# Windowed attention and two feed-forward networks on one core: the networks' instructions ordered by the in-kernel list scheduler

## The chip, the cores and the metric

One Trainium2 chip, one core. The metric is device time in microseconds (us) of the whole kernel. All times before and after are medians of several executions; the profile is one more execution.

## The reference

Inputs are float32; the kernel holds what attention makes and what the networks make on the chip.

```python
scores = q @ k.T / 8 + bias                 # 4 batches, 8 heads, 576 rows, head size 64
scores = where(0 <= rel < 128, scores, -1e9)
attn   = softmax(scores);  x = attn @ v     # x: 2304 tokens x 512
h = x @ w_in;  g = h * sigmoid(1.702 * h);  x = g @ w_out          # network 1: 512 -> 2048 -> 512
h = x @ w_in;  g = h if h >= 1, 0 if h <= -1, else (h + 1)**2 / 4  # network 2
out = g @ w_out
```

The four weight matrices come as float64 and are read by the kernel as pairs of int32.

## The kernel before

**Number format.** Each float32 operand of a product is split in a high part (float32r) and a low part, and a product is three matmuls (high·high, high·low, low·high). A slice of weights (128 x 512 numbers) is loaded as int32 pairs (`load_raw`, L256), turned into float32 by five steps (`convert`, L269: one on ScalarE, four on VectorE, lines 271 to 282), and split (L316 or L764 the high part on ScalarE, `low_of`, L291, the low part on VectorE or GpSimd).

**First product (the h stage).** Tokens come in three blocks of 768 for each network, so there are six blocks (`blk` 0 to 5). The inner width of 2048 is 16 slices, taken in 8 pairs. A pair of slices and a block's two halves are multiplied by a scheme with 7 products in place of 8 (`product`, L344; 6 matmuls each, L348). For it a pair of weights is made into five pieces A, B, C, E, F: four sums on GpSimd (`sum_w`, L305), a high part (L316) and a low part (L291) each. Four PSUM banks X, Y, Z, V hold partial results that are copied or added (L813, L359), then go through the activation (L366 or L368) and a multiplication (L372, or L375 and L376), which gives the tiles `g`. Pair `q` runs over all six blocks, 0 to 47.

**Second product (the o stage).** For each of 16 slices and two halves, `g` is split (L871, L291) and multiplied by the slice of `w_out`: 12 matmuls for network 1 (L911), 9 wider ones for network 2 (L913).

**Weights are prepared once.** In block 0 the pieces of network 1 are made and stored in DRAM (`keep_piece`, L729), likewise the split slices of `w_out` (L766). Blocks 1, 2 and later load them (L726, L866). Network 2's weights are prepared the same way in blocks 1 and 2 (`prepare_in`, L770, and `prepare_out`, L756), with loads and stores on GpSimd's queue and their tiles in a pool `tmp` of four buffers. A tile written to DRAM frees its buffer when the store has landed.

**What sets the order.** Every engine executes its queue in order and stops at a head that waits. For attention and pair 0 the queues are written by a planner: `jobs` (L57) lists jobs with an engine, an occupancy, a latency, needs, buffers taken and given, and a key; `in_order` (L181) repeatedly takes the job that can start earliest. In that part 10 slices (`EARLY`) of `w_in` of network 1 are also converted and stored in DRAM (`plain`), and pair 0 is read back and split. Everything behind it is issued by program order in the loop from L928: `stage_h` makes pair `q+1` while pair `q` is multiplied (`make_w`, L738, reads `plain` back), `to_plain` (L751) converts the six late slices into `plain`, and `background` (L922) puts in pieces of network 2's preparation by a fixed credit of 4 us for a pair and 2.4 us for a slice.

Of the kernel before, what the change touches and what calls it, by code (L numbers as in the profile page):

```python
# [12 lines left out]
F32 = mybir.dt.float32  # L13
# [4 lines left out]
EARLY = 10  # L18
# [31 lines left out]
SLACK, AHEAD = 26, 12  # L50
# [6 lines left out]
def jobs(nu, n_heads2, early):  # L57
# [5 lines left out]
    def load(name, eng, n, ns, key, takes=()):  # L63
        add(name, eng, 640 * n, 640, key, takes=takes)
        add((name[0] + " landed", name[1]), "DMA", ns, ns + 2000, key, [name])
# [70 lines left out]
    key = KEYS["pair"][0]  # L136
    add(("rd", 0), "SP", 640, 640, key - 4, [("ws landed", 0), ("ws landed", 1)], [("wraw", "rd")])
    add(("rd landed", 0), "DMA", 2400, 4400, key - 4, [("rd", 0)])
    for i in range(4):
        add(("cs", i), "POOL", 700, 830, key, [("rd landed", 0)] + [("cs", i - 1)] * (i > 0), [("sum", "w")] * (2 * (i == 0)))  # L140
    for i, (n, needs) in enumerate(((512, []), (512, [("cs", 3)]), (256, [("cs", 2)]), (256, [("cs", 3)]), (256, []))):
        add(("ch", i), "ACT", 90 + n, 220 + n, key, [("rd landed", 0)] + needs)
        add(("cl", i), "DVE", 50 + n * 3 // 2, 170 + n * 3 // 2, key, [("ch", i)] + needs,
            gives=[("wraw", "rd")] * (i == 4) + [("sum", "w")] * (2 * (i == 3)))
    key = KEYS["xs"][0]
    ready = [(x, u) for u in range(2 * n_heads2) for x in ("x0", "x1")]
    for i in range(4):
        needs = (ready, [("xt", 0)], ready + [("xt", 3)], [("xt", 1)])[i]
        add(("xt", i), "POOL", 1850, 2000, key + KEYS["xs"][1] * (0, 1, 3, 2)[i], needs, [("sum", "x")])
    for i in range(7):  # L150
        needs = ready if i < 3 else [("xt", (3, 0, 1, 2)[i - 3])] + [("xt", 1)] * (i == 4) + [("xt", 3)] * (i == 5)
        add(("xh", i), "ACT", 840, 970, key + KEYS["xs"][2] + KEYS["xs"][3] * i, needs)
        add(("xl", i), XL_ENG[i], *XL_COST[XL_ENG[i]], key + KEYS["xs"][2] + KEYS["xs"][3] * i, needs + [("xh", i)],
            gives=[("sum", "x")] * (i > 2))
    key = KEYS["h"][0]
    chain = []
    for n, (i, bank, needs) in enumerate((
            (1, "X", []), (5, "W", []), (6, "X", [("hc", "Y")]), (2, "Y", [("hc", "Y")]), (7, "X", [("hc", "Z")]),
            (3, "Z", [("hc", "Z")]), (4, "V", [("hc", "V")]))):
        tile_, part = A_OF[i]  # L160
        add(("h", i), "PE", 1060, 1260, key + 0.1 * n, needs + [("xl", B_OF[i]), ("cl", PIECE[tile_, part])] + chain[-1:],
            [("s", bank)] * (i in (1, 5)))
        chain = [("h", i)]
    for bank, i, need in (("Y", 1, ("h", 1)), ("Z", 6, ("h", 5)), ("V", 7, ("hm", 11))):
        add(("hs", bank), "PE", 180, 380, key + 0.1 * i, [need], [("s", bank)])
        add(("hc", bank), "DVE" if bank == "Z" else "ACT", 500, 640, key + KEYS["h"][1],
            [("h", i), ("hs", bank)] + [("hc", "W")] * (bank == "Z"))
# [822 lines left out]
```

## Time and profile before

| | us |
|---|---|
| median of 3 runs | 1012.98 (1010.64 to 1013.78) |
| the profiled execution | 1011.4 |
| its span, first to last instruction | 1009.6 |
| TensorE busy | 901.0 (89%) |
| VectorE busy | 650.9 (64%) |
| ScalarE busy | 485.2 (48%) |
| GpSimd busy | 239.2 (24%) |
| bytes moved | 223.44 MB, mean 221 GB/s |

The chain that ended last names TensorE for 54% of the span, transfers for 12% and VectorE for 12%. In the 40 slices, TensorE stands at 9 tenths from slice 23 on and at 6 to 8 in most of slices 6 to 22. The granted clock is 9 in most slices and 7 or 8 in some of slices 6 to 20. A stretch's "busy" time on TensorE counts matmuls at the clock of the moment, so a slower clock makes it longer.

### The profile page before, as it was taken

How to read it: one execution, taken by the hardware profiler on the slowest of the kernel's cores; microseconds unless marked ns; L12 is line 12 of the kernel's file. 1: busy time of each engine (PE TensorE's matmuls, PEld its weight loads, DVE VectorE, ACT ScalarE, POOL GpSimd, SP SyncE). 2: the span in 40 equal slices, each digit the busy share in tenths (PEclk: the TensorE clock that was granted, in tenths of full speed). 3: DMA queues.
4: the chain of work that ended last, by engine and by line, in shares of the span. 5: the costliest groups of instructions: out<-in, count | busy, mean ns of one | idle time of the engine just before them, and what ended most of it. 6: DMA issues, size and time to landing. Idle time of an engine off the chain costs nothing.

```text
span 1009.6 us, 17030 instructions
## 1 busy us (share of the span) xinstructions
PE 901.0 (89%) x6009; PEld 821.7 (81%) x6009; DVE 650.9 (64%) x1455; ACT 485.2 (48%) x1162; POOL 239.2 (24%) x361
## 2 busy tenths in 40 slices
PE   8987967776987886988777999999999999999998
PEld 6866857665976886987777889999889988899886
DVE  8979887667896655566677962679226772277421
ACT  6978955454444444333444632545225452355322
POOL 5759872432234332233311100000000000000000
PEclk9999979877999988999899999999999999999999
DMA  9996467666677887667899863676448853486233
GB/s 200 211 205 184 127 225 265 245 238 242 245 242 266 286 293 275 227 211 251 293 346 367 274 231 125 223 247 203 136 136 279 255 191 125 167 265 214 84 126 126
DMA packets 134726, 223.44 MB, mean 221 GB/s; under 512 B 65136, under 2 KB 73584, under 8 KB 134640
## 3 DMA queue, kind: packets, MB, share of 16 engines
q1 hardware_dynamic: 121248, 181.83, 56.7%
q0 software_dynamic: 11136, 39.85, 10.7%
q10 hardware_dynamic: 2256, 0.66, 0.3%
q8 instruction: 48, 0.79, 0.3%
q14 instruction: 38, 0.31, 0.1%
HBM read 167.25 MB, written 55.05 MB: 220 GB/s over the span
## 4 chain that ended last, share of the span: by engine, by line
PE 54%; DMA 12%; DVE 12%; issue 11%; POOL 7%; ACT 4%; SPq 0%; POOLq 0%; ACTq 0%; DVEq 0%
PE b L348 23%; PE b L913 19%; PE b L911 6%; DMA raw<-in_moe_w_out_dram 4%; POOL tmp L305 3%; PE ps_t L561 2%; PE ps_s L514 2%; PE ps_x L587 1%; DVE x L279 1%; DVE x L282 1%; PE ps_qk L494 1%; DVE gs L291 1%; DVE x L276 1%; DMA r<-plain 1%; DVE x L273 1%
## 5 line engine op out<-in xcount | busy, mean ns | idle before, releaser
L911 PE MATMUL b<-gs,wo 128*128 128x384 f32 x1152 | 211.9, 341 | 26.3 <-ACT gs L871 11.7
L911 PEld LDWEIGHTS b<-gs,wo 128*128 128x128 f32 x1152 | 201.5, 190 | 36.2 <-ACT gs L871 16.9
L291 DVE TENSOR_TENSOR gs<-g,gs 128x384 fp32r<-128x384 f32 x192 | 114.4, 599 | 143.7 <-ACT gs L871 143.3
L913 PE MATMUL b<-wo,gs 128*128 128x512 f32 x864 | 196.4, 389 | 0.0
L913 PEld LDWEIGHTS b<-wo,gs 128*128 128x128 f32 x864 | 162.1, 188 | 33.6
L871 ACT CAST gs<-g 128x384 fp32r<-128x384 f32 x192 | 96.9, 513 | 178.2 <-PE b L913 129.5
L348 PE MATMUL b<-xs,wB 128*128 128x384 f32 x564 | 124.8, 360 | 35.5 <-ACT b L813 29.4
L348 PEld LDWEIGHTS b<-xs,wB 128*128 128x128 f32 x564 | 106.4, 203 | 43.0 <-ACT b L813 33.9
L348 PE MATMUL b<-xs,wA 128*128 128x384 f32 x564 | 121.6, 351 | 14.7 <-ACT wA L316 7.5
L348 PEld LDWEIGHTS b<-xs,wA 128*128 128x128 f32 x564 | 105.1, 199 | 17.9 <-ACT wA L316 8.8
L368 ACT ACTIVATE g<-b,half 128x384 f32<-128x384 f32 x96 | 55.5, 584 | 46.0 <-PE b L348 44.9
L375 DVE TENSOR_TENSOR m<-b,g 128x384 f32<-128x384 f32 x96 | 53.2, 557 | 37.9 <-ACT g L368 35.9
L549 POOL TENSOR_SCALAR p<-p,sm 128x192 f32<-128x192 f32 (+2 forms) x144 | 63.9, 462 | 35.8 <-DVE sm L525 15.4
L359 DVE TENSOR_TENSOR b<-b,m 128x384 f32<-128x384 f32 x94 | 52.5, 559 | 29.0 <-PE b L348 24.4
L348 PE MATMUL b<-xs,wE 128*128 128x384 f32 x282 | 69.1, 340 | 0.0
L348 PE MATMUL b<-xs,wC 128*128 128x384 f32 x282 | 59.2, 345 | 11.1 <-DVE b L359 11.0
L533 ACT ACTIVATE p<-p,sm 128x192 f32<-128x192 f32 (+2 forms) x144 | 62.3, 441 | 7.0 <-DVE sm L525 6.9
L348 PEld LDWEIGHTS b<-xs,wC 128*128 128x128 f32 x282 | 50.6, 193 | 14.0 <-DVE b L359 14.0
L813 ACT COPY b<-b 128x384 f32<-128x384 f32 x94 | 44.0, 470 | 36.3 <-PE b L348 36.0
L372 DVE TENSOR_TENSOR g<-b,g 128x384 f32<-128x384 f32 x92 | 50.1, 554 | 16.1 <-ACT g L366 15.7
L348 PE MATMUL b<-xs,wF 128*128 128x384 f32 x282 | 57.9, 340 | 1.2 <-ACT b L813 1.2
L316 ACT CAST tmp<-tmp 128x256 fp32r<-128x256 f32 (+1 forms) x40 | 19.7, 491 | 77.7 <-POOL tmp L305 21.9
(168 smaller groups left out, 1248.8 us busy)
## 6 DMA issues: line engine op xcount, KB each, us to landing
wo<-r SPq DMA_DIRECT2D x80, 512.0 KB, 3.3
raw<-in_moe_w_in_dram SPq DMA_DIRECT2D x16, 512.0 KB, 4.9
raw<-in_moe_w_out_dram SPq DMA_DIRECT2D x16, 512.0 KB, 3.7
r<-wo SPq DMA_DIRECT2D x16, 512.0 KB, 3.0
raw<-in_moe_w_in_dram POOLq DMA_DIRECT2D x16, 512.0 KB, 5.5
raw<-in_moe_w_out_dram POOLq DMA_DIRECT2D x16, 512.0 KB, 5.7
r<-tmp POOLq DMA_DIRECT2D x16, 512.0 KB, 6.0
out_dram<-xt SPq DMA_DIRECT2D x17, 256.0 KB, 2.2
```

The costliest lines, as they stand in the source:

```text
L291: eng.tensor_tensor(out=dst[:, 1], in0=src, in1=f32(dst[:, 0]), op=ALU.subtract)
L348: nc.tensor.matmul(bank, wc[name][:, a, part, k * P:(k + 1) * P], xs[B_OF[i]][:, b, k, :], start=(first and k == 0 and n == 0), stop=(last ...
L359: nc.vector.tensor_tensor(out=dst, in0=bank, in1=m5, op=ALU.add)
L368: nc.scalar.activation(g, bank, AF.Relu, scale=0.5, bias=half)
L372: nc.vector.tensor_tensor(out=g, in0=bank, in1=g, op=ALU.mult)
L375: nc.vector.tensor_tensor(out=t, in0=bank, in1=g, op=ALU.max)
L533: nc.scalar.activation(x, x, AF.Exp, bias=sm[:, 0, a, e:e + 1], scale=-1.0, accum_out=sm[:, 1, a, e:e + 1])
L549: nc.gpsimd.tensor_scalar(out=x, in0=x, scalar1=st[u]["sm", g][:, 2, a, e:e + 1], scalar2=1.0, op0=ALU.mult, op1=ALU.mult)
L813: nc.scalar.copy(b, banks_of[q]["X"])
L871: nc.scalar.copy(gs[:, 0], g)
L911: nc.tensor.matmul(o[m][:, 0:N], wo[:, a, sl], gs[:, b, :], start=start, stop=stop)
L913: nc.tensor.matmul(o[m], gs[:, b, sl], wo[:, a, :], start=start, stop=stop)
```

## The change

The loop from L928 with its helpers is gone. A new function `ffn_jobs` lists every operation and every transfer of the six blocks as jobs with costs, and one call of `in_order` orders attention and networks together; the result is issued job by job. TensorE's own order of products is fixed by the list (look-ahead 1) and is the order that the loop had. For the other queues the look-ahead is 150 jobs; jobs of the networks take shared buffers in the order of their keys, and none is put on an engine before that engine's attention jobs are all placed.

```diff
-EARLY = 10
+EARLY = 8
-SLACK, AHEAD = 26, 12
+SLACK, AHEAD, AHEAD2 = 0, 12, 150
+LATE, SLACK2 = 1000, 100
+CAPS2 = dict(b=8, tmp=3, xtmp=1, wo=3, gs=3, m5=2, craw=2, cx=2)
+W_WORK = (("ACT", 690, 850), ("DVE", 440, 620), ("DVE", 430, 610), ("DVE", 710, 890), ("DVE", 700, 880))
+def ffn_jobs(nf, nj, early):
...
+    def move(name, eng, kb, at, needs=(), takes=(), gives=()):
+        add(name, eng, 450 if eng == "SP" else 700, 700, at, needs, takes)
+        add((name[0] + " landed", *name[1:]), "DMA", kb * 3, kb * 3 + (2500 if eng == "SP" else 4000), at, [name], (), gives)
...
+                    eng, occ = ("POOL", 1850) if x == 1 else ("DVE", 1100)
+                    add(name, eng, occ, occ + 160, t + 5500 * n - 1500, ...)   # the four differences of a block of x
...
+            move(("lw", q, x), "SP", size[x], first - 15000, needs)
...
+            eng, hold = eng_of(i), ["tmp" if i < 2 else "cx"] * (n == 2)
+            add(("ch", q, i), "ACT", 110 + size_, 280 + size_, t(i), needs, hold)
+            add(("cl", q, i), eng, occ, occ + 160, t(i) + 600, needs + [("ch", q, i)] + ...)
+            move(("kp", n, q % hp, i), "SP" if n == 1 else "POOL", 512 if size_ == 512 else 256, t(i) + 1500, [("cl", q, i)], (), hold)
...
+    for q in range(2, hp):
+        t = at["h", q, 1]
+        landed = [("rd landed", q)]
+        if 2 * q < early:
+            move(("rd", q), "SP", 512, t - 16000, (), ["wo"])
+        else:
+            for a in range(2):
+                conversion(1, 0, 2 * q + a, t - 14000 + 2500 * a, ["wo"] * (a == 0), "SP")
+            landed = [("w4", 1, 0, 2 * q + a) for a in range(2)]
+        sums(q, t - 8000, landed, ["tmp"])
+        pieces(q, 1, ..., "wo", lambda i: "POOL" if i < 1 else "DVE", landed)
...
+    begin, until = at["h", hp, 1], at["h", nj * hp, 1] - 10000
+    step = (until - begin) / hp      # network 2's pairs and slices are spaced by it
...
 def in_order(todo, caps):
...
-            for j in queue[:AHEAD]:
+            for j in queue[:AHEAD if not queue or queue[0].key < LATE else 1 if eng == "PE" else AHEAD2]:
+                if j.key >= LATE > queue[0].key:
+                    break
...
+                if j.key >= LATE and any(turns[what][0] != j.name for what in counts):
+                    continue
-                if first is None or (t <= first[0] + SLACK if j.key < first[1].key else t < first[0] - SLACK):
+                slack = SLACK if j.key < LATE else SLACK2
+                if first is None or (t <= first[0] + slack if j.key < first[1].key else t < first[0] - slack):
                     first = (t, j)
```

Late slices of `w_in` of network 1 (8 to 15) are converted straight into the tile from which their pair is split, without `plain`. Pairs 0 and 1 are both read back, summed and split in attention; pair 1 takes the buffers of attention's `raw` and `v` tiles. The low part of piece B of network 1 moves from GpSimd to VectorE, and the four differences of x for block 1 from VectorE to GpSimd. One pool of eight 4 KB buffers and one of five 2 KB buffers serve attention and the networks alike:

```diff
+    quad = keep_pool("quad", CAPS["raw"] + CAPS["wraw"] + CAPS["sum"])
+    duo = keep_pool("duo", CAPS["v"] + CAPS["wx"])
...
+    def do_ch(q, i):
+        name = NAMES[i]
+        if q < HP:
+            wcs.setdefault(q, {})[name] = new_wc(q, name)
+        else:
+            wcs.setdefault(q, {})[name] = (four if PARTS[name] == 2 else two)([P, 2, PARTS[name], 256], F32R, "piece")
+        high_w(i, wcs[q], sums_w.get(q), raw_in[q])
...
         with tc.manual_schedule():
-            for _, (what, *args) in in_order(jobs(NU, NP, EARLY), CAPS):
-                if what in do:
-                    do[what](*args)
+            for name in order:
+                if keys[name] < LATE and name[0] in do:
+                    do[name[0]](*name[1:])
...
+    with tc.manual_schedule():
+        for name in order:
+            if keys[name] >= LATE and name[0] in do:
+                do[name[0]](*name[1:])
```

The planner's keys for attention (`KEYS`) have new numbers throughout; the planner's costs of attention's jobs are the same but for loads that read `plain` back.

## Rows read from the trace of the kernel before

**Rows 1.** The page's first line.

```profile
span 1009.6 us, 17030 instructions
```

**Rows 2.** Stages: length; busy us (instructions) of PE, PEld, DVE, ACT, POOL; clock; DMA share, GB/s.

```profile
0.00:134.50 134.50, 118.81 (x2015) 97.09 (x2015) 116.92 (x518) 111.31 (x414) 92.65 (x183) 0.99 0.80 186
134.50:234.50 100.00, 68.24 (x299) 60.70 (x298) 72.90 (x113) 49.10 (x105) 42.47 (x42) 0.82 0.71 258
234.50:317.60 83.10, 74.68 (x384) 68.92 (x385) 66.97 (x102) 33.52 (x65) 30.51 (x26) 0.95 0.67 232
317.60:403.80 86.20, 66.34 (x337) 63.60 (x337) 51.54 (x100) 40.59 (x91) 26.19 (x37) 0.90 0.81 285
403.80:481.60 77.80, 69.15 (x386) 66.28 (x386) 48.73 (x86) 27.54 (x57) 25.67 (x36) 1.00 0.67 229
481.60:565.20 83.60, 65.24 (x339) 62.04 (x337) 60.11 (x117) 44.38 (x94) 17.38 (x31) 0.94 0.95 341
565.20:634.40 69.20, 67.43 (x386) 66.47 (x385) 40.26 (x71) 22.93 (x44) 4.38 (x8) 1.00 0.56 187
634.40:692.80 58.40, 58.40 (x337) 58.22 (x337) 42.32 (x81) 33.22 (x64) 0.00 (x0) 1.00 0.76 245
```

**Rows 3.** TensorE's timeline, the last unbroken run of block 2's o stage.

```profile
602.22 32.16 PE L911 MATMUL b<-gs,wo 128*128 128x384 f32 x184 [1.56 <-DVE gs L291]
```

**Rows 4.** Chain of waits from 120 to 150 us: start, length, what.

```profile
130.28 5.34 DMA r<-plain
...
135.68 2.85 POOL tmp L305 x3
```

**Rows 5.** TensorE's waits in block 0, 134.5 to 317.6: total, times, longest.

```profile
PE b L911 <- ACT wo L764: 7.8, 2, 7.6
PE b L348 <- ACT wA L316: 7.5, 4, 3.5
```

**Rows 6.** TensorE's waits in blocks 1 and 2, 317.6 to 634.4.

```profile
PE b L348 <- ACT b L813: 28.7, 10, 7.9
PE b L348 <- DVE b L359: 9.3, 5, 3.4
```

**Rows 7.** ScalarE's waits in the same stretch.

```profile
ACT x L271 <- DMA raw<-in_moe_w_out_dram: 34.1, 12, 4.6
ACT tmp L316 <- POOL tmp L305: 17.6, 5, 4.2
...
ACT tmp L316 <- DMA r23A<-tmp: 6.1, 1, 6.1
...
ACT tmp L316 <- DMA r20A<-tmp: 4.1, 1, 4.1
```

**Rows 8.** The page's DMA issues: count, KB, median us from issue to landing.

```profile
raw<-in_moe_w_in_dram POOLq DMA_DIRECT2D x16, 512.0 KB, 5.5
```

**Rows 9.** VectorE by line and form, 317.6 to 634.4: busy us, mean ns, idle before.

```profile
L291 DVE TENSOR_TENSOR gs<-g,gs 128x384 fp32r<-128x384 f32 x64 | 37.6, 596 | 22.9 <-ACT gs L871 22.8
L372 DVE TENSOR_TENSOR g<-b,g 128x384 f32<-128x384 f32 x64 | 34.9, 553 | 10.2 <-ACT g L366 10.0
L279 DVE SCALAR_TENSOR_TENSOR x<-raw,x 128x512 int32<-128x512 int32 x16 | 11.0, 685 | 0.1
L291 DVE TENSOR_TENSOR tmp<-tmp 128x256 fp32r<-128x256 f32 x24 | 10.2, 424 | 32.1 <-ACT tmp L316 32.0
L291 DVE TENSOR_TENSOR xs<-tmp,xs 128x768 fp32r<-128x768 f32 x8 | 7.6, 952 | 0.3 <-ACT xs L339 0.3
L273 DVE TENSOR_SCALAR x<-x 128x512 f32<-128x512 f32 x16 | 6.9, 430 | 17.0 <-ACT x L271 17.0
```

**Rows 10.** Two forms where GpSimd is busy: VectorE 134.5 to 234.5, GpSimd whole trace.

```profile
L279 DVE SCALAR_TENSOR_TENSOR x<-raw,x 128x512 int32<-128x512 int32 x9 | 8.2, 906 | 0.1
L333 POOL TENSOR_TENSOR sum<-xt 128x768 f32<-128x768 f32 x2 | 4.1, 2042 | 0.0
```

**Rows 11.** One stretch of block 2, columns as in rows 2.

```profile
500.00:525.00 25.00, 19.84 (x102) 18.88 (x101) 17.08 (x35) 12.23 (x27) 3.60 (x7) 0.93 0.98 362
```

More of the change, by code (lines that the diff above doesn't have):

```diff
@@ L135, in jobs @@
         add(("ws landed", f), "DMA", 1400, 3400, key + KEYS["w"][5], [("ws", f)], gives=[("wx", f)])
[L136 to L144, printed above, removed]
+    for p in range(2):
+        key = KEYS["pair"][p]
+        load(("rd", p), "SP", 2, 2600, key - 4, [("wraw", "rd")], [("ws landed", 2 * p), ("ws landed", 2 * p + 1)])
+        for i in range(4):
+            add(("cs", p, i), "POOL", 740, 870, key, [("rd landed", p)] + [("cs", p, i - 1)] * (i > 0),
+                [("sum", "w")] * (i == 0))
+        for i, (n, last) in enumerate(((512, None), (512, 3), (256, 2), (256, 3), (256, None))):
+            needs = [("rd landed", p)] + [("cs", p, last)] * (last is not None)
+            takes = [("raw", "w")] * (p == 1 and i < 2) + [("v", "w")] * (p == 1 and i > 1)
+            add(("ch", p, i), "ACT", 105 + n, 250 + n, key, needs, takes)
+            add(("cl", p, i), "DVE", 50 + n * 3 // 2, 170 + n * 3 // 2, key, [("ch", p, i)] + needs,
+                gives=[("wraw", "rd")] * (i == 4) + [("sum", "w")] * (i == 3))
     key = KEYS["xs"][0]
@@ new lines, in jobs @@
+            needs = [("hp", 0)]
+        add(("ha", 0, c), "ACT", 550 + 1300 * (n == 0), 680 + 1300 * (n == 0), key + KEYS["h"][2] + 0.1 * n, needs + last
+            + [("ha", 0, 11)] * (n > 0))
+        add(("hm", 0, c), "DVE", 560, 700, key + KEYS["h"][2] + 0.1 * n, [("ha", 0, c)], gives=[("s", bank)])
+    return out
+LATE, SLACK2 = 1000, 100
+CAPS2 = dict(b=8, tmp=3, xtmp=1, wo=3, gs=3, m5=2, craw=2, cx=2)
+W_WORK = (("ACT", 690, 850), ("DVE", 440, 620), ("DVE", 430, 610), ("DVE", 710, 890), ("DVE", 700, 880))
@@ L186, in in_order @@
     free = {what: [0] * n for what, n in caps.items()}
+    turns = {}
+    for j in sorted(todo, key=lambda j: j.key):
+        for what in {what for what, _ in j.takes} if j.key >= LATE else ():
+            turns.setdefault(what, []).append(j.name)
     seen, shape, order = {}, None, []
@@ L210, in in_order @@
         shape = j.name[0] if j.eng == "PE" else shape
+        for what in {what for what, _ in j.takes} if j.key >= LATE else ():
+            turns[what].pop(0)
         for what, _ in j.takes:
@@ L256, in load_raw @@
     def load_raw(n, i, f, queue=nc.sync):
-        raw = stage.tile([P, 512, 2], I32, tag="raw", name="raw")
+        raw = four([P, 512, 2], I32, "raw")
         src = weights[n][i]
@@ L266, in new_x @@
     def new_x():
[L267 removed]
+        return two([P, 512], I32, "x")
     def convert(step, raw, x):
@@ new lines, in do_xt, with xs_of, do_xh @@
+    def do_xt(blk, i):
+        held = (blk, {1: 0, 3: 1}.get(i))
+        sums_x[blk, i] = sums_x[held] if blk and held in sums_x else four([P, 2, N], name="sums")
+        sum_x(i, blk % NJ, {n: sums_x.get((blk, n)) for n in (0, 1, i)}, nc.vector if blk > 1 else nc.gpsimd)
+    def xs_of(blk, i):
+        return {n: sums_x.get((blk, n)) for n in range(4)}
+    def do_xh(blk, i):
+        if blk:
+            xss.setdefault(blk, {})[i] = new_xs(i)
+        high_x(i, blk % NJ, xss[blk], xs_of(blk, i))
@@ new lines, in do_xl @@
+    def do_xl(blk, i):
+        eng = nc.vector if blk or XL_ENG[i] == "DVE" else nc.gpsimd
+        low_x(i, blk % NJ, xss[blk], xs_of(blk, i), eng)
+    common = dict(h=do_h, hc=do_hc, hp=do_hp, ha=do_ha, hm=do_hm, cs=do_cs, ch=do_ch, cl=do_cl, xt=do_xt, xh=do_xh, xl=do_xl)
+    NJ = NT // (2 * N)
+    NB = 2 * NJ
+    HP = NF // 2
+    opened, m5_of, g_more = [], {}, {}
+    todo = jobs(B * NP, NP, EARLY) + ffn_jobs(NF, NJ, EARLY)
+    keys = {j.name: j.key for j in todo}
+    order = [name for _, name in in_order(todo, {**CAPS, **CAPS2})]
```

627 lines of the change are left out of this document (306 added, 321 removed).

## The prediction

> **What bounds the kernel now.** I read the page's head first [rows 1], then a table of stages cut where TensorE begins another block's work [rows 2], then who TensorE waited for in the stages where it isn't full [rows 5, 6], and last what held the engine that it waited for [rows 7].
>
> The table is the main view. From 634.4 us to the end at 1009.6 us (375.2 us) TensorE is never without work: an h stage takes 58.4 us and is 58.40 us busy. That row is the floor of any h stage: 8 pairs, so 7.3 us a pair. An o stage of network 1 has 384 matmuls; 184 of them run unbroken in 32.16 us [rows 3], so its floor is 384 x 0.174 = 66.8 us. Against these floors the first 634 us stand so:
>
> - attention with pair 0, 134.5 us; no floor is known, VectorE is busy 116.92 us (87%), ScalarE 111.31 (83%);
> - block 0, pairs 1 to 7 and the o stage: 100.0 + 83.1 = 183.1 us against 7 x 7.3 + 66.8 = 117.9;
> - blocks 1 and 2: 86.2 + 77.8 + 83.6 + 69.2 = 316.8 us against 2 x (58.4 + 66.8) = 250.4.
>
> So 65.2 + 66.4 = 131.6 us can be lost time of TensorE, and none of it lies behind 634.4 us. The reader is to see also that a part of it is a slow clock: between 134.5 and 234.5 us the granted clock is 0.82 and 299 matmuls are busy 68.24 us, which at the unbroken rate are 52. TensorE had waited before, so this returns with the waits.
>
> In block 0 the wait is for weights being made: after attention the read of `plain` takes 5.34 us and three sums 2.85 us before pair 1 can be split [rows 4], and TensorE waits for split pieces and for the first slice of the second product [rows 5]. In blocks 1 and 2 the h stages lose 86.2 + 83.6 - 116.8 = 53.0 us, the o stages 13.4. The waits there are for a bank copy on ScalarE, 28.7 us, and a bank add on VectorE, 9.3 us [rows 6], together 38.0. ScalarE isn't short of time (40.59 of 86.2 us); it stands behind background work: for raw weights of network 2, 34.1 us; for sums, 17.6; and for a `tmp` buffer whose last content is still on its way to DRAM [rows 7]. Seven rows for the stores of piece A, 6.1 down to 4.1, make 35.6 us, and all 19 rows of such stores 50.5.
>
> **The change part by part.** I sum by stages, against the execution profiled.
>
> *Attention.* It gives up two slices to convert: two 0.685 and two 0.430 steps each [rows 9], 2 x 2.22 = 4.4 us of VectorE. It takes on pair 1: two low halves of 512 columns (0.69, like the steps of that width) and three of 256 (0.424), 2.7 us. So VectorE has 1.7 us less of 117 and no engine much more. The read-back of pair 1 and its sums move in from where they stood alone [rows 4], beside attention's own work; without that cover they would cost 5.34 + 2.85 + some 2 us again. The new keys reorder everything here, and nothing in the trace prices that. The bounds are 128 (the two slices and a few waits go) and 145 (pair 1's 10 us are not hidden). I take 134, nearest to the row.
>
> *Block 0.* Here VectorE is the limit. Its work after the change, at the durations of the stretch where GpSimd is quieter [rows 9]: 28 gate products x 0.553 = 15.5; 14 bank adds x 0.56 = 7.8; 8 + 16 slices x 2.22 = 53.3; low halves of 6 pairs x (0.69 + 3 x 0.424) = 11.8 (B comes over from GpSimd); 7 splits of x, 0.952 each, 6.7; 32 splits of g x 0.596 = 19.1; 4 evacuations, 2.2. Sum 116. The same list for before (26 slices, 31 splits of g, 4 differences of x, 3 low halves a pair) gives 124, and the trace shows 72.90 + 66.97 = 139.9, 1.13 times as much: beside a busy GpSimd one step takes 906 ns in place of 685 [rows 10]. GpSimd loses B's halves and gains the four differences, so I keep the ratio: 116 x 1.13 = 131 us, above TensorE's 117.9. An engine is never full in a queue that waits; VectorE is 87% busy in attention, the part that the planner orders, and 73 and 81% in block 0 [rows 2]. At 87% block 0 takes 151 us, at 95% 138, at 82% 160. I take 146 (90%), nearer to the planner's row, and keep 131 and 160 as ends. The transfers fit: the stages moved 258 GB/s x 100 us + 232 x 83.1 = 45 MB, the late slices save the write and read of `plain`, 6 x 2 x 0.26 = 3 MB, and 42 MB in 146 us are 288 GB/s, below the 362 of [rows 11]. The saved round trip itself I cost at nothing: the slice must still be loaded and converted by the same steps.
>
> One rule speaks against a piece of this. The step of 685 ns takes 906 beside GpSimd's work, and over block 0 73 us of GpSimd's time cost VectorE 16 us, 0.22 for each. Four differences of x on GpSimd at 2.04 us [rows 10] then cost VectorE 1.8 us and save it 3.8. The Trainium skill (SBUF — State Buffer, section "SBUF: two separate sides") says that VectorE and GpSimd share a port pair by an exclusive lock that whoever starts first holds for the whole instruction. By that the four could block VectorE for 8.2 us, and the move would lose 4.4 us in place of gaining 2. The trace agrees that there is a price, not that it is the whole instruction; the sum goes by the trace.
>
> *Blocks 1 and 2.* TensorE's 250.4 us stay. Stores: pieces C, E, F go to the small buffers and A, B to the large, and a copy is put on ScalarE's queue only where the plan has its buffer free. That is where the 50.5 us go, and most of the 17.6 for sums, since copies come when the plan has them ready. What stays is a load that lands later than planned. Of 102 us of background waits (34.1 + 17.6 + 50.5) a third stays, and I let a third of the lost time stay: 18 of 53.0 in the h stages, 4 of 13.4 in the o stages. 250.4 + 22 = 272 us. Bounds: 255 (a plan kept almost exactly) and 316 (nothing gained). What is late next is VectorE or the transfers. VectorE: 51.54 + 48.73 + 60.11 + 40.26 = 200.6 us, plus 6 for the two slices and the pair that network 2 no longer gets done in block 0, is 76% of 272. Transfers: 285 x 86.2 + 229 x 77.8 + 341 x 83.6 + 187 x 69.2 = 84 MB, plus 3 moved from block 0, at 362 GB/s [rows 11] 240 us, 88% of 272. Three things near their limits are why I don't go to 255.
>
> *From block 3 on.* The order is TensorE's own and its partners are half idle, so 375.2 us; preparation now runs up to 10 us before block 3 by its keys, where it had ended by 600, and I add 2 us, with 0 and 8 as ends. Buffers shared by number cost nothing where the counts are the old ones, as they are here (8 of 4 KB, 5 of 2 KB).
>
> Sum: 134 + 146 + 272 + 377 = 929 us of span. The execution profiled took 1011.4 us, 1.8 above its span, and the median of the runs 1.6 more: 929 + 3.4 = 932 us.
>
> **The rivals.**
>
> *The plan holds* (better than I think): VectorE at 98% in block 0 (133 us), 257 in blocks 1 and 2, 375.2 behind: 134 + 133 + 257 + 375 + 3.4 = 902. For it: the look-ahead of 150 jobs finds work for any gap. Against it: planned latencies are constants, and in the trace loads spread.
>
> *Transfers bound the h stages.* Blocks 1 and 2 reach 285 and 341 GB/s in the h stages already, against 229 and 187 in the o stages [rows 2]; if preparation stays in the h stages, these keep 86 + 84 us, the o stages go to 137, block 0 to 155, the end to 379: 134 + 155 + 307 + 379 + 3.4 = 978. Against it: the 362 of [rows 11] held for that whole stretch, and a plan that counts transfers as one server moves them. The Trainium skill (DMA: Bandwidth & Descriptors, section "Measured") gives 425 GB/s for one core with large transfers; by it 87 MB need 205 us and this rival falls away. No stretch of 25 us that I read moves more than about the 362 of [rows 11], so it keeps its chance.
>
> *Slower: heads that wait.* The planner takes the job that can start earliest, and ties alone go by key, so each background step stands in ScalarE's and VectorE's queues at the very moment that its load is planned to land, with bank copies right behind it. The change has 26 loads to wait for in block 0, 32 in blocks 1 and 2, and 56 stores that free buffers: 114. In the h stages TensorE lost 38.0 us for 102 us of ScalarE's background waits, 0.37 for each. To eat up the floor's 131.6 us each transfer must be 131.6 / (114 x 0.37) = 3.1 us later than planned on average. At 3.6 us: 134.5 + 117.9 + 250.4 + 375.2 + 152 + 3.4 = 1033. For it: the read-back took 5.34 us [rows 4] and the plan gives 4.0 (512 KB x 3 ns + 2.5). Against it: a load by GpSimd's queue takes 5.5 us [rows 8], and the plan gives 5.5.
>
> *It doesn't do what it says*: pair 1 isn't done within attention, because ScalarE is 83% and VectorE 87% busy there, and the 10 us of [rows 4] come back at its end: 942.
>
> **How the numbers follow.** Forecast 0.54, the plan holds 0.16, transfers 0.11, pair 1 not hidden 0.03, heads that wait 0.16. The measurement can tell 0.3% (3 us) from no change; of the last case a quarter, with lateness near 3.1 us, falls within that. So faster 0.54 + 0.16 + 0.11 + 0.03 = 0.84, the same 0.04, slower 0.12. The time is the forecast's, 932 us. The range takes in the plan that holds down to 895 and the transfers up to 985; it leaves out the last case and the best part of the first, about 0.2.
>
> **What would show it.** In the changed kernel's stages: block 0 near 146 us with VectorE near 90%; blocks 1 and 2 near 272 us with no row of a ScalarE wait for a store of piece A; no read of `plain` between attention and pair 1; a granted clock near 1.00 after 134 us; 375 us for the last three blocks. The prediction is wrong if ScalarE's waits for loads grow beyond the 34.1 us, if block 0's VectorE share stays near 75%, or if attention moves by more than 10 us.

## The result and the profile after

The changed kernel takes 931.47 us (median of four runs, 928.35 to 938.87), beside 1011.81 us (1009.0 to 1013.78) for the kernel before on the same chip: a ratio of 0.9218, with a 95% interval of 0.9156 to 0.9281. That is 80 us, or 7.8%, faster. The forecast was 932.0. The execution that left the profile took 933.57 us, 1.8 above its span.

The page's head answers to [rows 1]: total time, the busy time of each engine, and the chain of waits by engine.

```profile
span 931.8 us, 16987 instructions
PE 881.4 (95%) x6010; PEld 810.4 (87%) x6010; DVE 657.8 (71%) x1459; ACT 488.6 (52%) x1162; POOL 233.4 (25%) x357
PE 69%; DVE 10%; DMA 8%; issue 5%; POOL 4%; ACT 2%; SPq 1%; POOLq 0%; ACTq 0%; DVEq 0%
```

TensorE's busy time fell by 20 us although it does the same products: that is less time at the slow clock. VectorE is busy 7 us longer, and TensorE's part of the chain rose from 54 to 69%. So TensorE's work is the same, and what left the span is waiting and slow clock.

The table of stages answers to [rows 2], cut again where TensorE begins another block's work. The columns are the window, its length, busy time and count of TensorE, weight loads, VectorE, ScalarE and GpSimd, the granted clock, the share of the DMA engines, and GB/s.

```profile
0.00:136.10 136.10, 121.69 (x2016) 97.92 (x2017) 115.06 (x517) 112.68 (x418) 97.97 (x190) 0.96 0.79 189
136.10:200.70 64.60, 55.25 (x301) 51.26 (x300) 58.60 (x110) 41.29 (x94) 30.02 (x30) 1.00 0.86 303
200.70:281.60 80.90, 73.13 (x386) 68.69 (x386) 73.03 (x104) 39.18 (x72) 31.39 (x22) 0.96 0.66 236
281.60:343.50 61.90, 59.59 (x338) 58.06 (x337) 44.92 (x84) 34.23 (x75) 15.26 (x24) 1.00 0.93 329
343.50:410.20 66.70, 66.70 (x386) 66.70 (x385) 51.96 (x89) 32.10 (x61) 17.49 (x28) 1.00 0.80 282
410.20:481.00 70.80, 63.23 (x337) 61.91 (x336) 46.73 (x89) 35.48 (x76) 15.31 (x25) 0.93 0.95 336
481.00:547.80 66.80, 66.80 (x386) 66.48 (x384) 51.95 (x85) 31.37 (x61) 18.68 (x30) 1.00 0.76 266
...
547.80:614.90 67.10, 62.03 (x337) 60.90 (x338) 55.71 (x105) 35.39 (x72) 7.32 (x12) 0.95 0.83 286
614.90:931.80 316.90, 313.00 (x1537) 278.51 (x1536) 159.82 (x282) 126.87 (x239) 0.00 (x0) 1.00 0.51 173
```

The reader sees four things. Both o stages of blocks 1 and 2 are at the floor of 66.8 us. Their h stages take 61.9 and 70.8 us where they took 86.2 and 83.6. Block 0 behind pair 0 takes 145.5 us in place of 183.1. And the h stage of block 3, the last but one row, takes 67.1 us where it took 58.40; everything behind it is as it was, 316.9 us. Lost time of TensorE against its floors is now 145.5 - 117.9 = 27.6 us in block 0 and 266.2 - 250.4 = 15.8 us in blocks 1 and 2. That returns 88.2 of the 131.6 us; 8.8 are given back from block 3 on and 1.6 in attention, which leaves the 77.8 us between the spans.

Who held TensorE, which answers to [rows 5, 6]: engine and line that waited, what released it, total us, times, longest. First block 0, behind the dots blocks 1 and 2, last block 3 to the end.

```profile
PE b L539 <- ACT wB L505: 4.3, 3, 1.7
PE b L990 <- ACT wo L953: 4.3, 2, 2.9
PE b L539 <- DVE wB L477: 3.1, 4, 1.8
PE b L990 <- POOL wo L477: 2.4, 5, 0.8
...
PE b L539 <- DVE b L550: 3.6, 2, 2.9
PE b L539 <- DMA wA<-r17A: 3.0, 1, 3.0
PE b L539 <- DMA wA<-r14A: 2.2, 2, 1.6
PE b L539 <- DMA wA<-r12A: 1.1, 1, 1.1
...
PE b L539 <- DVE b L550: 4.7, 2, 4.1
```

In blocks 1 and 2 the 28.7 us for a copy on ScalarE are gone and 3.6 us for an add on VectorE are left of 9.3. What is late next is the load of a stored piece, 6.3 us, of which 4.6 us fall in the h stage of block 2, with a DMA share of 0.95. What ScalarE itself stood behind, in block 0 (two rows) and in blocks 1 and 2, answers to [rows 7]:

```profile
ACT wo L953 <- DVE x L473: 24.7, 14, 3.7
ACT x L462 <- DMA raw<-in_moe_w_out_dram: 8.1, 3, 3.6
...
ACT raw L953 <- DVE x L473: 9.8, 5, 2.4
ACT r L462 <- DMA raw<-in_moe_w_in_dram: 8.5, 4, 2.5
ACT piece L505 <- DMA r20A<-piece: 2.7, 1, 2.7
ACT piece L505 <- DMA r21F<-piece: 2.7, 1, 2.7
ACT piece L505 <- DMA r23F<-piece: 2.1, 1, 2.1
```

In blocks 1 and 2 raw loads hold it for 8.5 us in place of 34.1, stores for 8.4 in place of 50.5 (the three rows shown and one of 0.9), and sums no longer stand in the list. One wait for the store of a piece A (2.7 us) is left of seven.

### The profile page after: what moved, and what is told of

Read it like the earlier page. It is cut to its first block, busy times and chain, and to the rows that moved or that the text cites. A ratio compares the mean times of both kernels' runs of the same rounds, so it can differ in the third digit from the quotient of the medians.

```text
span 931.8 us, 16987 instructions
## 1 busy us (share of the span) xinstructions
PE 881.4 (95%) x6010; PEld 810.4 (87%) x6010; DVE 657.8 (71%) x1459; ACT 488.6 (52%) x1162; POOL 233.4 (25%) x357
## 4 chain that ended last, share of the span: by engine, by line
PE 69%; DVE 10%; DMA 8%; issue 5%; POOL 4%; ACT 2%; SPq 1%; POOLq 0%; ACTq 0%; DVEq 0%
PE b L539 28%; PE b L992 21%; PE b L990 12%; PE ps_s L788 2%; DMA wA<-r14A 2%; PE ps_x L861 2%; PE ps_t L835 2%; DMA raw<-in_moe_w_out_dram 1%; DVE x L470 1%; POOL sums L494 1%; PE ps_qk L768 1%; DVE x L464 1%; DVE gs L477 1%; DMA wA<-r17A 1%; DVE x L473 1%
## 5 line engine op out<-in xcount | busy, mean ns | idle before, releaser
L990 PE MATMUL b<-gs,wo 128*128 128x384 f32 x1152 | 206.7, 339 | 7.8 <-ACT wo L953 4.3
L539 PE MATMUL b<-xs,wB 128*128 128x384 f32 x576 | 119.2, 341 | 9.8 <-ACT wB L505 4.3
L539 PE MATMUL b<-xs,wA 128*128 128x384 f32 x576 | 118.7, 341 | 6.7 <-DMA wA<-r17A 3.0
L539 PEld LDWEIGHTS b<-xs,wB 128*128 128x128 f32 x576 | 102.3, 191 | 14.2 <-ACT wB L505 5.7
L539 PEld LDWEIGHTS b<-xs,wA 128*128 128x128 f32 x576 | 103.0, 192 | 8.7 <-DMA wA<-r17A 3.3
L823 POOL TENSOR_SCALAR p<-p,sm 128x192 f32<-128x192 f32 (+1 forms) x144 | 63.6, 459 | 36.9 <-DVE sm L818 23.3
L563 DVE TENSOR_TENSOR g<-b,g 128x384 f32<-128x384 f32 x96 | 52.2, 550 | 23.5 <-ACT g L557 22.9
L807 ACT ACTIVATE p<-p,sm 128x192 f32<-128x192 f32 (+1 forms) x144 | 62.3, 439 | 5.3 <-DVE sm L799 5.2
L557 ACT ACTIVATE g<-b 128x384 f32<-128x384 f32 x96 | 46.4, 491 | 34.8 <-PE b L539 32.6
L539 PE MATMUL b<-xs,wE 128*128 128x384 f32 x288 | 58.6, 338 | 0.0
```

Source lines behind the costliest of these rows:

```text
L539: nc.tensor.matmul(bank, wc[name][:, a, part, k * P:(k + 1) * P], xs[B_OF[i]][:, b, k, :], start=(first and k == 0 and n == 0), stop=(last ...
L557: nc.scalar.activation(g, bank, AF.Sigmoid, scale=1.702)
L563: nc.vector.tensor_tensor(out=g, in0=bank, in1=g, op=ALU.mult)
L807: nc.scalar.activation(x, x, AF.Exp, bias=sm[:, 0, a, e:e + 1], scale=-1.0, accum_out=sm[:, 1, a, e:e + 1])
L823: nc.gpsimd.tensor_scalar(out=x, in0=x, scalar1=st[u]["sm", g][:, 2, a, e:e + 1], scalar2=1.0, op0=ALU.mult, op1=ALU.mult)
L990: nc.tensor.matmul(o[m][:, 0:N], wo[:, a, sl], gs[:, b, :], start=start, stop=stop)
```

## The experiments

Times are medians; ratios are to the kernel before in the same series. The four stages are read from each run's one profile. Attention is cut where pair 0's products end, the others at the first matmul of a stage (so a wait ahead of it counts to the stage before; this moves 0.4 us between the last two columns for the change).

| | us | ratio (95%) | attention, pair 0 | block 0 | blocks 1, 2 | block 3 on |
|---|---|---|---|---|---|---|
| before | 1011.81 | 1 | 134.5 | 183.1 | 316.8 | 375.2 |
| the change | 931.47 | 0.9218 (0.9156 to 0.9281) | 136.1 | 145.4 | 266.7 | 383.6 |
| the change, again | 928.65 | 0.9175 (0.9132 to 0.9217) | 134.5 | 146.3 | 264.4 | 383.3 |
| pair 1 late | 935.64 | 0.9222 (0.9189 to 0.9255) | 133.6 | 152.8 | 259.5 | 383.6 |
| order by key | 957.66 | 0.9448 (0.9418 to 0.9478) | 134.3 | 150.6 | 295.3 | 374.9 |
| a step left out, same plan | 927.87 | 0.9150 (0.9126 to 0.9174) | 136.8 | 141.8 | 263.8 | 383.3 |
| a step left out, planned anew | 919.91 | 0.9094 (0.9067 to 0.9121) | 132.8 | 140.8 | 261.0 | 382.0 |
| before, C, E, F in small buffers | 1004.10 | 0.9913 (0.9871 to 0.9955) | 133.6 | 184.6 | 313.7 | 375.1 |
| preparation ends earlier | 924.83 | 0.9137 (0.9116 to 0.9158) | 136.0 | 146.8 | 264.0 | 376.3 |
| differences on VectorE | 929.02 | 0.9186 (0.9156 to 0.9216) | 133.2 | 149.3 | 260.5 | 382.7 |
| landings 1.5 us sooner in the plan | 936.70 | 0.9272 (0.9224 to 0.9321) | 134.7 | 146.6 | 272.2 | 379.7 |
| round trip put back | 933.59 | 0.9233 (0.9191 to 0.9276) | 134.6 | 154.5 | 261.0 | 383.1 |
| earlier end, landings 1 us later | 935.88 | 0.9249 (0.9200 to 0.9298) | 136.8 | 152.8 | 262.1 | 384.9 |
| earlier end, B on GpSimd | 923.25 | 0.9127 (0.9088 to 0.9166) | 134.8 | 147.5 | 263.3 | 376.2 |

The two series of the change itself lie 3 us apart, so I read nothing from totals that differ by less. Single executions of one kernel lie further apart (928.35 to 938.87 us for the change), and a profile is one execution: stages that differ by a few us between two profiles are weak evidence.

**The change, again.**

> The changed kernel once more, beside the next three on the same chip: 931 us (928 to 939 in its four runs so far). By the stages of its profile: attention with pair 0 136 us, block 0 145.5, blocks 1 and 2 266, from block 3 on 384.

The total is the same within the intervals, and each stage within 2.3 us. This is the row that the variants are held against.

**Which pick orders the queues.** The look-ahead picks the job that can start first. Here it picks by key among jobs that start within 4 us.

```diff
-LATE, SLACK2 = 1000, 100
+LATE, SLACK2 = 1000, 4000
```

> The changed kernel, but among the networks' jobs a job with an earlier key (its due time) goes ahead of one that could start up to 4 us sooner, where the change lets it go ahead only within 0.1 us. Jobs, buffers and TensorE's order stay. Theory (the gain in blocks 1 and 2 is that no queue head waits where other work could run): heads wait up to 4 us again; ScalarE's waits for loads, stores and sums in blocks 1 and 2 grow from some 30 us to 60 or more, blocks 1 and 2 from 266 us to 280 to 300, block 0 by 3 to 10, the whole to 948 to 975. Rival (any order made from due times does it, the gain is from the buffers and the spacing of the background work): within 5 us of 931.

Blocks 1 and 2 take 295.3 us, 29 to 31 more. TensorE's waits there:

```profile
PE b L539 <- DVE b L550: 13.2, 6, 4.6
PE b L990 <- DVE gs L477: 6.8, 6, 2.8
PE b L539 <- ACT b L601: 6.6, 7, 1.9
```

The adds and copies of banks are back as the rows that hold TensorE, as in [rows 6]: a job taken for its key stands at the head before its input is there, and ScalarE's waits for raw loads are 24.4 us in place of 8.5 and those for stores 26.6 in place of 8.4, together 51 where I had expected 60 or more. The theory held: of 50 us gained in blocks 1 and 2, some 29 hang on the pick of the earliest start. The same run gives 374.9 us from block 3 on, 8 to 9 less, as its preparation had ended before block 3. So the whole grows by less, 23 to 28 us by the ratios.

**Buffers alone.** The kernel before, with the three smaller pieces taken from the small buffers, as the change does.

```diff
-            w = {name: temp([P, 2, PARTS[name], 256], F32R)}
+            shape = [P, 2, PARTS[name], 256]
+            w = {name: temp(shape, F32R) if PARTS[name] == 2 else stage.tile(shape, F32R, tag="x", ...)}
```

> The kernel before, with one part of the change alone: pieces C, E and F of network 2's pairs are made in the two small buffers of the converted slices, not in the four large background buffers, so that they don't wait for the store of piece A. Order and everything else are as before. Theory (the store waits held ScalarE's queue and with it the bank copies): the seven waits for the stores of A, 35.6 us, and most of the 50.5 us of all go; at 0.37 us of TensorE for each, blocks 1 and 2 fall from 316.8 to some 300 us, the whole from 1012 to 993 to 1000. Rival (the order is what counts: a head freed of one wait stands in the next): less than 5 us, 1007 or more, with the waits moved to loads or sums.

It gains 9 us in the median; the profiled execution, the slowest of the five with a span of 1007.0 us, shows 3.1 in blocks 1 and 2 and no gain behind them. ScalarE's waits there:

```profile
ACT x L271 <- DMA raw<-in_moe_w_out_dram: 30.5, 11, 5.6
...
ACT piece L316 <- DMA r27C<-piece: 6.9, 1, 6.9
```

Of the seven waits for stores of piece A one is left (3.7 us), but waits for the other kind of load (11.6 us) and seven for stores of C (20.4 us in all, the longest shown) have come in, and TensorE still waits 20.2 us for bank copies (28.7 in [rows 6]). So a cause of ScalarE's waits was removed and the next one took its place. The 9 us lie between the two expectations; these buffers in the old order give a small part of the gain, and the run doesn't say what they give in the new one.

**The price of late transfers.** The plan counts each landing 1.5 us sooner, so that every head waits longer.

```diff
-(2500 if eng == "SP" else 4000)
+(1000 if eng == "SP" else 2500)
```

> The changed kernel with the planner told that every transfer of the networks lands 1.5 us sooner than the change has it (1.0 and 2.5 us behind its bytes in place of 2.5 and 4.0), so that each background step stands in its queue that much too early. This puts a price on the rival of heads that wait. Rival as priced in the prediction (0.37 us of TensorE for each us that a queue head waits, 114 transfers): 114 x 1.5 x 0.37 = 63 us, the whole 985 to 1000. Theory (most transfers have slack in the plan, a late one holds the queue only where the next step was due at once): ScalarE's waits for raw weights in blocks 1 and 2 grow by 20 to 40 us, TensorE loses 5 to 20, the whole 935 to 950.

Total +5 to +8 us, blocks 1 and 2 +5.5 to +7.8, ScalarE's waits for raw loads 13.4 us in place of 6.4 in the second profile of the change. By the price in the prediction, 114 transfers x 1.5 us x 0.37 would have cost 63 us. That price does not hold. ScalarE's waits grew by 5 to 7 us, not by the 20 to 40 of my theory, so I take it that most of the added lateness falls where nobody stands behind it; that was not followed transfer by transfer.

**The end of preparation.** It was set 10 us ahead of block 3's start by key; here 45 us.

```diff
-    begin, until = at["h", hp, 1], at["h", nj * hp, 1] - 10000
+    begin, until = at["h", hp, 1], at["h", nj * hp, 1] - 45000
```

> The changed kernel with network 2's background work spaced to end 45 us before block 3 in place of 10 us. In the changed kernel the last pair's steps still run up to 30 us into block 3, whose h stage takes 66 us against 58.4. Theory (the missed term of the sum is this spill): from block 3 on 375 to 377 us in place of 384, blocks 1 and 2 266 to 271, the whole 923 to 929. Rival (blocks 1 and 2 have no room, VectorE and the transfers being near their limits): blocks 1 and 2 grow by 8 us or more, the whole 931 or slower.

Block 3 on takes 376.3 us in place of 383.3 to 383.6, blocks 1 and 2 stay at 264.0, and the total falls by 4 to 7 us (the intervals of the totals touch; the stage is the clearer sign). The h stage of block 3, same columns as the stage table:

```profile
546.80:605.20 58.40, 57.34 (x329) 56.76 (x329) 45.77 (x89) 31.63 (x64) 2.69 (x5) 1.00 0.82 283
```

It is back near its floor with 10 us less of VectorE's work in it (45.77 against 55.71). The theory held.

**Later landings with it.** The same edit, and landings planned 1 us later (3500 and 5000 ns).

> The changed kernel with network 2's work spaced to end 45 us before block 3 (924.8 us alone) and the planner told that transfers land 1 us later than the change has it (3.5 and 5.0 us behind their bytes). Theory (in the trace loads by GpSimd's queue land 5.3 to 6.2 us after issue where the plan has 5.5, so a margin takes waits away): blocks 1 and 2 256 to 262 us in place of 264, the whole 915 to 922. Rival (a margin holds buffers longer in the plan and only moves work later): 923 to 930.

It is 11 us slower than the edit alone, in block 0 (+6.0) and from block 3 on (+8.6). Blocks 1 and 2 gained 1.9 us, the whole lost more than either expectation had. The margin pushes work back: the last step of preparation on GpSimd's queue begins 47 us into block 3, where it began 13 us into it with the earlier end alone. In block 0 TensorE's waits for the low halves of B on VectorE rose from 3.2 to 6.2 us.

**Pair 1 in attention, undone.** Pair 1 is again read back, summed and split behind attention, as pairs 2 and 3 are; its slices are still converted in attention.

```diff
-    for p in range(2):
+    for p in range(1):
...
-    for q in range(2, hp):
+    for q in range(1, hp):
```

> The changed kernel, but pair 1 is read back, summed and split behind attention, by the list of the networks' jobs, as pairs 2 and 3 are. Theory (preparing pair 1 within attention took away a wait at its end): the read of 5.3 us, sums of 2.9 us and a first split of some 2 us stand between pair 0 and pair 1 again, 7.3 us of pair 0's products cover part; attention with pair 0 keeps 136 us or loses up to 3, block 0 grows from 145.5 to 150 to 156 us, the whole from 931 to 936 to 942. Rival (the planner finds cover for it wherever it stands): block 0 grows by less than 2 us, the whole stays within 3 us of 931.

Block 0 takes 152.8 us, 6.5 to 7.4 more, and attention 0.9 to 2.5 less. The end of block 0, where both parts count, is 286.4 us against 281.5 and 280.9: pair 1 in attention is worth about 5 us there, half of the 10 that I had put on it. By the ratios the total is the same as the change's: blocks 1 and 2 came out 5 to 7 us shorter in this profile, and why is open; it was the fastest of the four executions, 4 us under their median.

**VectorE in block 0, first with the plan kept.** The step of L464 is not issued for the conversions of network 1; the plan still counts it.

```diff
+        if step != 1 or n == 2:
             convert(step, raws[n, i, f], xw[n, i, f])
```

> The changed kernel without one of the four VectorE steps of converting a slice (the step that bounds the magnitude), for the 24 slices of network 1 that are converted behind attention: that part of the computation is left out. In block 0 these steps are busy 17.7 us (10.3 us at the 0.43 us of a quiet stretch). Theory (VectorE is the limit of block 0, 131.6 us busy of 145.5): block 0 shortens by 8 to 16 us, to 129 to 137, VectorE's share stays near 0.9; the whole 915 to 923. Rival (what ends the waits in block 0 is the chain of load, steps and split of each slice, or the transfers at 303 GB/s): block 0 shortens by 3 us or less, VectorE's share falls to 0.8.

VectorE is busy 13 us less in block 0 (118.4 of 131.6), and block 0 is 3.6 to 4.5 us shorter, a little more than the rival's 3. VectorE's share fell to 0.84, so its work alone didn't set the pace. The h stage, same columns as the stage table (0.7 us of it still belong to pair 0):

```profile
136.10:200.95 64.85, 58.39 (x305) 54.87 (x304) 54.94 (x100) 42.03 (x96) 29.11 (x31) 0.95 0.85 301
```

There VectorE is busy 3.7 us less than in the change, and the stage is 0.5 to 1.5 us shorter. But a kept plan can hide part of the gain, so the step was also taken out of the plan.

```diff
+            if n == 1 and step == 1:
+                continue
```

> The run without the bounding step for network 1's 24 slices behind attention, but with the step also left out of the planner's list, so that the queues are ordered anew for it. With the old order block 0 went from 145.5 to 142.5 us and VectorE's share from 0.90 to 0.84. Theory (VectorE is the limit, the old order kept what it freed from being used): block 0 131 to 137 us, the whole 917 to 924. Rival (VectorE isn't the limit; the chain load, steps, split on ScalarE and GpSimd, and a half clock after each wait are): block 0 140 to 144 us again, the whole 925 to 929.

The two rows of block 0, h stage and o stage:

```profile
133.00:198.01 65.01, 56.44 (x300) 52.68 (x299) 58.39 (x101) 40.62 (x93) 30.69 (x31) 0.97 0.87 303
198.01:273.63 75.62, 70.33 (x385) 65.87 (x385) 65.61 (x88) 38.10 (x72) 29.61 (x21) 1.00 0.72 253
```

VectorE is busy 7.4 us less and block 0 takes 4.6 to 5.5 us less, at a share of 0.88, nearly all of it in the o stage. There VectorE's busy time fell by 7.4 us and the stage by 5. In the h stage its busy time didn't fall (58.39 us, 58.60 in the change), so this run doesn't test it there. At 140.8 us block 0 lies in the rival's range (140 to 144), the whole in the theory's. VectorE counts in the o stage; in the h stage, by the run with the kept plan, something else limits.

**The round trip put back.** The late slices of network 1 are again written to DRAM and read back. Both landings are planned; the slice gets a small buffer for the conversion, and to make room for the trip the conversion is due 10 us earlier.

```diff
-                conversion(1, 0, 2 * q + a, t - 14000 + 2500 * a, ["wo"] * (a == 0), "SP")
+                conversion(1, 0, 2 * q + a, t - 24000 + 2500 * a, ["cx"], "SP")
+                move(("wp", 1, 0, 2 * q + a), "SP", 256, ...)
+            move(("rd", q), "SP", 512, ...)
```

> The changed kernel with one part undone: the eight late slices of network 1 are converted into a small buffer, stored to DRAM and read back before their pair is split, as the kernel before did; all of it stands in the planner's list. Theory (the prediction cost the saved round trip at nothing): block 0 145 to 149 us, the whole 929 to 935. Rival (the h stage of block 0 moves 303 GB/s already and two more landings of 2.3 and 4.5 us stand in each pair's chain): block 0 grows by 5 to 12 us, the whole 935 to 945.

The h stage of block 0:

```profile
134.60:208.50 73.90, 60.93 (x301) 57.10 (x300) 60.45 (x112) 42.78 (x95) 28.34 (x30) 0.91 0.91 324
```

It takes 73.9 us in place of 64.6 and 65.6, with 324 GB/s and a granted clock of 0.91, while VectorE's work over block 0 is not more (130.2 us). So block 0 as a whole is 8 to 9 us longer in this profile, as the rival had it. By the total 2 to 5 us are left, within the intervals, since blocks 1 and 2 were again shorter.

Not all of it can be put down to the trip. GpSimd's sums wait 23.9 us for the slices that are read back, where in the change they wait 13.6 us for converted ones; that is the trip. But TensorE's longest wait in the stage is for a bank add on VectorE:

```profile
144.85 2.19 PE L540 MATMUL b<-xs,wC 128*128 128x384 f32 x6 [3.86 <-DVE b L551]
```

Ahead of that add VectorE does eight conversion steps, from 137.2 us on, 2.6 us behind pair 0's end; in the change the first comes 6.8 us behind it. That goes with the earlier due time. Nor is bandwidth shown to be the cause: in the run of later landings with the earlier end the h stage takes 73.0 us as well, at 275 GB/s and without the trip.

**Differences of x on VectorE.** The four differences for block 1, which are made during block 0, go back from GpSimd.

```diff
-                    eng, occ = ("POOL", 1850) if x == 1 else ("DVE", 1100)
+                    eng, occ = "DVE", 1100
```

> The changed kernel with the four differences of x for block 1 back on VectorE, from GpSimd. Theory (the price by the trace: 3.8 us more of VectorE's work, 1.8 less of its delay beside GpSimd): block 0 0 to 3 us longer, the whole 931 to 935. Rival (an exclusive lock for the whole instruction, as the Trainium skill has it in SBUF — State Buffer, section SBUF: two separate sides): VectorE's steps beside these four lose up to 8.2 us on GpSimd, so block 0 gets 2 to 5 us shorter, the whole 926 to 929.

The two rows of block 0, h stage and o stage, and behind them TensorE's longest wait there:

```profile
133.00:197.76 64.76, 55.42 (x303) 51.45 (x301) 58.82 (x110) 41.59 (x95) 30.22 (x30) 1.00 0.86 304
197.76:282.55 84.79, 73.34 (x385) 68.53 (x385) 70.17 (x108) 38.91 (x72) 27.93 (x18) 0.96 0.65 228
```

```profile
PE b L990 <- POOL wo L477: 9.2, 8, 4.0
```

58.82 + 70.17 = 129.0 us, against 131.4 in the second profile of the change, although VectorE does 4 x 0.95 = 3.8 us more. So 8.4 us on GpSimd (4.3 + 4.1 for the four) had cost VectorE some 6.2 us; it is a difference of two orders, in which other steps stand beside GpSimd too. The trace of the change shows the cost itself. Two of the four differences, each with the VectorE step that it caught:

```profile
218.93 2.13 POOL L524 TENSOR_TENSOR sums<-xt,sums 128x768 f32<-128x768 f32 x1 [2.97 <-DVE xs L477]
219.30 2.03 DVE L464 TENSOR_SCALAR x<-x 128x512 f32<-128x512 f32 x1
...
234.74 2.03 POOL L524 TENSOR_TENSOR sums<-xt 128x768 f32<-128x768 f32 x1
234.99 2.20 DVE L477 TENSOR_TENSOR gs<-g,gs 128x384 fp32r<-128x384 f32 x1
```

With no work of GpSimd beside them these steps take 0.42 and 0.55 us. Here they begin 0.4 and 0.2 us after a difference has begun, and end 0.3 and 0.4 us after it has ended. The other two differences catch a step each in the same way (1.95 us for 0.42, 1.28 for 0.55). Together that is 5.5 us for the 8.4.

Still block 0 is 3 to 4 us longer: TensorE waits 9.2 us for GpSimd's low halves, 2.8 before, and these take 1.70 us each where they took 1.39. So VectorE's time went as the rival had it, and block 0 as the theory had it. The total is the same.

**B on GpSimd, with the earlier end.**

```diff
-lambda i: "POOL" if i < 1 else "DVE"
+lambda i: "POOL" if i < 2 else "DVE"
```

> The changed kernel with network 2's work spaced to end 45 us before block 3 (924.8 us alone) and the low half of piece B of network 1 back on GpSimd. VectorE loses 6 x 0.73 = 4.4 us of work in block 0 and gains delay beside 6 x 1.4 = 8.4 us more of GpSimd's: 1.8 us at the prediction's 0.22 for each, 6.2 us at the 0.74 that the four differences showed. At 0.22: block 0 1 to 3 us shorter, the whole 921 to 924. At 0.74: block 0 the same or up to 3 us longer, as GpSimd's own steps (1.4 us against 0.73) stand in the chain, the whole 925 to 929.

923.25 us, the same as the earlier end alone within the intervals. Block 0 isn't shorter (147.5 us, 146.8 with the earlier end alone). The total fits the price of 0.22 and block 0 that of 0.74; VectorE's busy time in block 0 tells more. It is 129.8 us, 130.5 with the earlier end alone; so by the difference of two orders again, of 4.4 us of work taken away 3.7 came back as delay, beside 8.0 us of B's halves on GpSimd: 0.46 for each us. The two versions with the earlier end are the best that compute everything: 4 to 8 us below the change, and 88 us (ratio 0.9127) below the kernel before for this one.

## Why the prediction was right, and where it wasn't

The total was within 1 us, which is luck, since errors in single stages cancel: by the profile I was 7 us too low from block 3 on and 2 in attention, and 6 too high in blocks 1 and 2.

*Block 0, 146 forecast, 145.4 measured.* VectorE was forecast at 131 us and 90%; the rows show 58.60 + 73.03 = 131.6 us and 90.5%. The numbers hold, the reason only in part. In the o stage VectorE counts: with 7.4 us of its busy time taken away the stage gave back 5, and 24.7 us of ScalarE's waits for a conversion step stand in block 0, nearly all in that stage. In the h stage it isn't the limit that I took it for: 3.7 us less of it gave back 0.5 to 1.5 us. What limits there stays open. TensorE waits there mainly for the split of B, 4.3 us for its high and 3.1 us for its low halves; the 303 GB/s are less than the 329 and 336 of later h stages. The step "the saved round trip costs nothing" is in doubt as well: I counted bytes, 42 MB in 146 us, as a mean over both stages, and they are not even (303 GB/s in the h stage, 236 in the o stage), and each trip adds two landings to the way of a slice to its pair. With the trip put back block 0 was 8 to 9 us longer. How much of that is bandwidth, the two landings, or the earlier conversions was not taken apart.

*The rule on the port.* I priced GpSimd's time at 0.22 us of VectorE's for each us; for the four differences the two runs give 6.2 / 8.4 = 0.74 and the rows of the change's trace 5.5 / 8.4 = 0.66. The Trainium skill (SBUF — State Buffer, section "SBUF: two separate sides") says that whoever holds the shared port holds it for the whole instruction, which I had worked out as 8.2 us. The measurement is much nearer to that than to my 1.8. The rows show it too: a step caught by a difference ends only after it. My 0.22 was too low as a mean as well. I set a list of durations against busy time, but a step begins before the one ahead of it has ended, and in block 0 before the change the durations add up to 9 us more than the busy time. If each step of block 0 is held against steps of its form that met nothing on GpSimd, those beside it are 27.6 us longer in the change's trace, for 59.3 us of GpSimd's arithmetic. That is 0.47 for each us, an estimate from single instructions. The move of the differences thus lost 1.7 to 2.4 us of VectorE's time in place of saving 2. Block 0 didn't show it, since undone it made TensorE wait for GpSimd's low halves.

*Pair 1.* It is multiplied right behind pair 0 in the trace, with no read of `plain` between, so the rival "it doesn't do what it says" fell. Its worth was 5 us at the end of block 0, not 10, since undone TensorE waited 1.1 and 1.8 us for it behind pair 0: a part of its preparation found cover. Attention came out at 136.1 and 134.5, with 134 forecast.

*Blocks 1 and 2, 272 forecast, 266.2 measured.* I let a third of the 102 us of background waits stay; 8.5 + 8.4 = 16.9 us did, a sixth, and the o stages lost nothing where I had left 4. The mechanism was right (order by key gives 29 us back), but for one sign: a wait for a store of piece A was left. Of the 15.8 us still lost, 9.9 are the waits shown and the rest the slower clock behind them.

*From block 3 on, 377 forecast, 384.0 measured.* This is the mis-sized term. I saw that preparation may run on by its keys and gave it 2 us, with 8 as the end; it cost 8.8 us, all in one h stage. The timelines (start, us, engine, line, tile) show how, VectorE first:

```profile
568.10 0.69 DVE L477 TENSOR_TENSOR raw<-x,raw 128x512 fp32r<-128x512 f32 x1
568.71 1.11 DVE L477 TENSOR_TENSOR piece<-sums,piece 128x512 fp32r<-128x512 f32 x2
569.74 0.55 DVE L566 TENSOR_TENSOR m<-b,g 128x384 f32<-128x384 f32 x1
...
570.80 0.56 DVE L550 TENSOR_TENSOR b<-b,m 128x384 f32<-128x384 f32 x1
...
571.41 2.29 PE L539 MATMUL b<-xs,wC 128*128 128x384 f32 x6 [4.06 <-DVE b L550]
573.50 2.12 PE L539 MATMUL b<-xs,wA 128*128 128x384 f32 x6
575.41 2.04 PE L539 MATMUL b<-xs,wB 128*128 128x384 f32 x6
577.30 1.21 PE L539 MATMUL b<-xs,wE 128*128 128x384 f32 x6
```

The last low halves of network 2 (`raw`, `piece`) stand on VectorE ahead of the bank add that TensorE waits for; the wait is 4.06 us, and these steps are 1.7 us of it. VectorE is busy through all of it, behind conversion steps of network 2 before. Then three groups of six matmuls run at half speed: they begin 5.89 us before the fourth, where at full speed groups begin 1.04 us apart, so another 2.8 us go. Waits (4.7) and slow clock make up 7.5 of the 8.7 us of that stage. Moving the end 35 us earlier gave 7 back.

*The rivals.* "Transfers bound the h stages" was seen in small: 329 and 336 GB/s at shares of 0.93 and 0.95, and 6.3 us of waits for pieces. It didn't decide, because preparation went on into the o stages, at 282 and 266 GB/s where they had 229 and 187. Nor are the 362 GB/s, which I took for about the most, a ceiling: one slice of 23 us in the page of the change moves 385. "Heads that wait" fell with the run of sooner landings. "The plan holds" was reached in the o stages only; no version came near 902. What stays open is why near-identical variants differ by 4 to 7 us in blocks 1 and 2 (259.5 to 266.7); an order that changes everywhere with each key is my guess, not shown, and the totals of single executions of one kernel differ by as much.

## What to carry to other kernels

In engines that execute in order, put a background step into a queue at the moment when its inputs are planned to be there, not by when it is due: the pick alone was worth 29 us in two blocks here (23 to 28 of the whole), and small buffers in the old order 9. Then look at the stage in which the background work ends: it must end before the stage that had no slack, and 35 us of key made 7 us there. And count transfers by stage, not as a mean over two.

## What the hardware showed

A two-input operation on GpSimd held up VectorE steps until it had ended: a step of 0.42 us that began 0.4 us after a difference of 2.13 us took 2.03 us. The price for each us on GpSimd was 0.66 to 0.74 us of VectorE's time for the four differences and 0.46 for the low halves of B; I had put it at 0.22. The gate products, which read a bank, didn't pay: 18 of 31 ran beside GpSimd's work in block 0, and they took 0.55 us as the others did.

TensorE's clock fell to its lower level after short waits. Behind the wait of 4.06 us the granted clock was 0.51 of full speed for 5.9 us, which is the 1.2 GHz level, and then 1.00. In the slower h stage of block 2 groups of six matmuls take 2.29 us, in place of 1.20, behind waits of 2.94 and 2.96 us, and 1.32 us behind one of 1.63 us. The length of a wait alone doesn't decide it: in the run with the round trip a group took 2.21 us behind a wait of 1.50 us. The wait of 4.06 us cost 1.7 times itself: (4.06 + 2.8) / 4.06.
